# Hash-masked attention feeding an RWKV channel mix: second pair in query halves, third pair turned by TensorE, PSUM banks written out per operation, a new written sequence

## The chip, the cores and the metric

The kernel runs on one core of a Trainium2 chip (trn2). The metric is the device time of one execution in microseconds. The kernel before was timed three times: 250.73, 250.70 and 248.66 us, median 250.7.

Engines are named as in the profile: PE (matrix products), PEld (its weight loads), DVE (vector), ACT (scalar, activations), POOL (GpSimd), SP (here a queue that issues DMAs). PSUM is the accumulator memory that PE writes: 8 banks of 512 float32 a partition.

## The reference, cut to what matters

```python
# q, k, v: 4 batches x 8 heads x 768 positions x 64; proj: 64 x 6
q_bucket = sum over 6 bits of (q @ proj > 0) * 2**bit          # the same for k
scores = where(q_bucket == k_bucket, q @ k.T / 8, -1e9)
attn = exp(scores - max) / (sum + 1e-9)
x = (attn @ v) with the 8 heads side by side                   # 4 x 768 x 512
x_prev = x shifted by one position, zeros first
xk = mu_k * x + (1 - mu_k) * x_prev                            # xr the same with mu_r
out = sigmoid(xr @ w_r) * (relu(xk @ w_k) ** 2 @ w_v)          # w_k 512x1024, w_v 1024x512, w_r 512x512
```

## The kernel before

**Tiling.** Two heads make a pair; there are 16 pairs, four to a batch, and the channel mix (MoE in the names) of a batch runs once its four pairs are done. The code builds a list of operations with data dependencies (`add`, L144); a list of numbers, `ORDER` (L70), says in which sequence they are written, and each engine executes its own in that sequence, waiting where a dependency asks for it. `WHERE` (L40) gives the engine of the operations that may run on several. `Plan.schedule` (L199) walks through `ORDER` with estimated costs in order to choose PSUM banks: scores take a pair of banks out of three pairs, everything else one of banks 7 to 3.

**A pair, step by step.** The names in quotation marks are those of the operations; n is the pair.

- "ldq", "ldv": SP loads q and k (`nat`) and v (`vn`).
- "hi", "lo": q and k are split into two 16-bit halves, side by side in `nh`. For pairs in `FIRSTS` (0 and 1) it is done head by head, 384 columns a time (hi L616 on ACT or L618, lo L621); for the others 768 at a time (hi L554 or L556, lo L559). lo reads `nat` and the hi half of `nh`.
- Turning `nh` into `a` (64 + 64 rows, positions along the columns): for pairs in `FIRSTS` by six PE transposes a head ("t", L635) and a copy out of PSUM ("evt", L639); for the others by two DMA transposes ("tr", L563), issued by SP.
- The bucket bits: pair 0 has its own matmuls and evictions for each head and side ("b" L657, "beb" L663 on ACT, L665 on DVE). The others have 24 matmuls ("bits", L587), one eviction ("bx", L591) and 2 or 4 DMAs that carry the bits to rows of `a` ("row", L599, issued by SP). A score of equal buckets gets a constant that the exponential's bias takes off again.
- "sc" (L708): nine steps of 128 x 1024 scores; "exp" (L712): nine ACT exponentials into `pt`.
- "oo" (L736, L741): 72 matmuls of 65 columns, probabilities times v with a column of ones; "rc" (L751) and "ob" (L758) divide by the sum.
- The result is turned again, by PE ("ot" L794, copied out by "xt" L798) for pairs 0 to 3 and 15, by a DMA for the rest, then "xs", "xj" (shift by one), "df" L829, "xka", "xra" L837 and "xk", "xr" L841 form the mixed inputs on DVE.

Pairs in `HALVED` (2 and 3) run in two query halves: scores, "oo", "rc", "ob", "ot", "xt" and the mix are split, so that the first half of the positions goes on before the second.

**A batch's channel mix.** "kp" (L859, 16 groups of 4 matmuls of 384 columns), "relu" (L864 on ACT, L866 on DVE), "sq" (L869), "r" (L884) with "tanh" (L887), "v" (L896, eight matmuls of 512), "os" (L903) and the store "st" (L907). The last tile ("v3_5") is done in two column halves, lo and hi, which share a bank.

**Other things that are touched.** The weights come by "wl" (L447) and are cast by "wc" (L450 to L452). mu_k and mu_r are loaded element by element by ACT's queue (L422) and reduced by one on DVE (L424). v sums ("vsum", L509 to L515) and casts ("va", L501) run on POOL or DVE. Seven matmuls on zeros (L390) open PE's work.

Of the kernel before, what the change touches and what calls it, by code (L numbers as in the profile page):

```python
# [16 lines left out]

LAG = {"PE": 0.21, "ACT": 0.21, "DVE": 0.15, "POOL": 0.18, "SP": 1.8, "GQ": 2.0}
# [17 lines left out]
def R(kind, n):  # L36
# [33 lines left out]
ORDER = [  # L70
# [65 lines left out]
class Plan:  # L136
# [7 lines left out]
    def add(self, eng, dur, prio, fn, r=(), w=(), take=None, give=(), lag=None, name="", at=0.0, svc=0.0, off=None, tr=0, port=0, land=1.5):  # L144
# [31 lines left out]
        self.ops.append(o)  # L176
        return o

    def sequence(self):
        if ORDER:  # L180
            return [self.ops[i] for i in ORDER]
        left = {o.i: len(o.deps) for o in self.ops}
# [3 lines left out]
        while heap:  # L186
            o = self.ops[heapq.heappop(heap)[1]]
            seq.append(o)
            for s in o.succ:
                left[s] -= 1  # L190
                if not left[s]:
                    heapq.heappush(heap, (self.ops[s].prio, s))
# [772 lines left out]
```

## Time and profile before

| profiled execution | value |
|---|---|
| span, first to last instruction | 251.3 us (the three timed runs: median 250.7) |
| PE busy | 236.9 us, 94%, 2609 matmuls |
| DVE busy | 195.4 us, 78%, 471 instructions |
| ACT busy | 179.1 us, 71%, 225 instructions |
| POOL busy | 27.9 us, 11%, 73 instructions |
| chain that ended last | PE 75%, DMA 11%, DVE 8%, SP queue 3% |
| 144 exponentials (L712) | 138.8 us, 1040 ns each |
| 28 lo of 768 columns (L559) | 27.3 us, 976 ns each |
| 22 hi of 768 columns on DVE (L556) | 12.3 us, 557 ns each |

The profile is one execution. "Busy" is the time in which an engine had an instruction under way; idle time is put down to the instruction or DMA that released the next one. The chain is followed back from the last instruction, at each step to what released it.

### The profile page before, as it was taken

How to read it: one execution, taken by the hardware profiler on the slowest of the kernel's cores; microseconds unless marked ns; L12 is line 12 of the kernel's file. 1: busy time of each engine (PE TensorE's matmuls, PEld its weight loads, DVE VectorE, ACT ScalarE, POOL GpSimd, SP SyncE). 2: the span in 40 equal slices, each digit the busy share in tenths (PEclk: the TensorE clock that was granted, in tenths of full speed). 3: DMA queues.
4: the chain of work that ended last, by engine and by line, in shares of the span. 5: the costliest groups of instructions: out<-in, count | busy, mean ns of one | idle time of the engine just before them, and what ended most of it. 6: DMA issues, size and time to landing. Idle time of an engine off the chain costs nothing.

```text
span 251.3 us, 6510 instructions
## 1 busy us (share of the span) xinstructions
PE 236.9 (94%) x2609; PEld 147.6 (59%) x2609; DVE 195.4 (78%) x471; ACT 179.1 (71%) x225; POOL 27.9 (11%) x73
## 2 busy tenths in 40 slices
PE   6886799999799998999999999999999999999993
PEld 2444578876566655666467566655865654545442
DVE  3795679889788889898998999899787878376322
ACT  5596689999799978996878899988787223332220
POOL 5002240541302031100001100100000000000000
PEclk9799799999999999999999999999999999999998
DMA  6999999999989999999999996793231030022223
GB/s 187 308 178 251 220 215 191 267 249 189 213 292 241 204 293 292 273 201 269 184 333 186 184 185 158 210 230 57 90 64 44 0 128 28 13 83 86 83 85 125
DMA packets 75194, 44.56 MB, mean 177 GB/s; under 512 B 55524, under 2 KB 70172, under 8 KB 75164
## 3 DMA queue, kind: packets, MB, share of 16 engines
q1 hardware_dynamic: 74028, 44.15, 72.8%
q8 instruction: 20, 0.33, 0.6%
q10 hardware_dynamic: 1136, 0.01, 0.3%
q14 instruction: 10, 0.08, 0.1%
HBM read 24.12 MB, written 6.29 MB: 121 GB/s over the span
## 4 chain that ended last, share of the span: by engine, by line
PE 75%; DMA 11%; DVE 8%; SPq 3%; ACT 1%; issue 1%; DVEq 0%
PE ps_all L708 19%; PE ps_all L896 17%; PE ps_all L859 13%; PE ps_all L741 12%; PE ps_all L884 8%; DMA nat<-in_k_dram 5%; PE ps_all L587 4%; DMA nat<-in_q_dram 3%; DMA a<-bx 2%; DMA os<-in_moe_w_k_dram 1%; DVE nh L559 1%; DVE nh L556 1%; PE ps_all L736 1%; ACT pt L712 1%; PE ps_all L794 1%
## 5 line engine op out<-in xcount | busy, mean ns | idle before, releaser
L712 ACT ACTIVATE pt<-ps_all 128x1024 bf16<-128x1024 f32 x144 | 138.8, 1040 | 21.1 <-PE ps_all L708 19.8
L708 PE MATMUL ps_all<-a 128*128 128x512 f16 (+3 forms) x408 | 80.6, 318 | 5.1 <-DMA a<-bx 3.9
L708 PEld LDWEIGHTS <-a 128*128 128x128 f16 x408 | 35.3, 98 | 26.7 <-DMA a<-bx 4.7
L859 PE MATMUL ps_all<-xk,wk 128*128 128x384 bf16 x256 | 49.0, 326 | 0.9 <-DVE kr L866 0.9
L896 PE MATMUL ps_all<-wv,k 128*128 128x512 bf16 (+1 forms) x200 | 45.9, 370 | 0.6 <-DVE os L903 0.6
L741 PEld LDWEIGHTS <-pt 128*128 128x128 bf16 x1152 | 42.1, 98 | 6.9 <-issue 1.1
L741 PE MATMUL ps_all<-va,pt 128*128 128x65 bf16 x1152 | 43.9, 194 | 0.0
L859 PEld LDWEIGHTS <-wk 128*128 128x128 bf16 x256 | 24.5, 98 | 17.6 <-issue 1.6
L896 PEld LDWEIGHTS <-k 128*128 128x128 bf16 x200 | 19.4, 98 | 20.6 <-issue 0.7
L864 ACT ACTIVATE kr<-ps_all 128x384 bf16<-128x384 f32 x33 | 15.8, 493 | 19.2 <-DVE k L869 12.7
L887 ACT ACTIVATE rs<-ps_all 128x512 f32<-128x512 f32 x24 | 14.2, 603 | 20.9 <-PE ps_all L884 19.0
L559 DVE SCALAR_TENSOR_TENSOR nh<-nat,nh 128x768 f16<-128x768 f32 x28 | 27.3, 976 | 1.1 <-ACT nh L554 0.6
L903 DVE SCALAR_TENSOR_TENSOR os<-rs,ps_all 128x512 f32<-128x512 f32 (+1 forms) x25 | 16.5, 662 | 14.7 <-PE ps_all L896 9.9
L869 DVE TENSOR_TENSOR k<-kr 128x384 bf16<-128x384 bf16 x64 | 21.5, 350 | 3.7 <-ACT kr L864 3.5
L884 PE MATMUL ps_all<-wr,xr 128*128 128x512 bf16 x96 | 23.8, 379 | 0.0
L866 DVE TENSOR_SCALAR kr<-ps_all 128x384 bf16<-128x384 f32 x31 | 17.1, 555 | 8.3 <-PE ps_all L859 6.6
L758 DVE TENSOR_TENSOR ob<-ps_all,rc 128x384 bf16<-128x384 f32 (+1 forms) x36 | 18.3, 511 | 1.0
L884 PEld LDWEIGHTS <-xr 128*128 128x128 bf16 x96 | 9.0, 98 | 10.0 <-ACT kr L864 0.3
L587 PE MATMUL ps_all<-a,p0g 128*32 128x256 f16 (+1 forms) x180 | 13.4, 276 | 1.3 <-DMA a<-nh 1.3
L556 DVE TENSOR_SCALAR nh<-nat 128x768 f16<-128x768 f32 x22 | 12.3, 557 | 3.0 <-DMA nat<-in_q_dram 2.5
L587 PE MATMUL ps_all<-a,p1g 128*32 128x256 f16 (+1 forms) x180 | 12.9, 273 | 0.0
L841 DVE TENSOR_TENSOR xr<-tm,xt 128x768 bf16<-128x768 f16 (+1 forms) x18 | 9.4, 520 | 0.4
(94 smaller groups left out, 187.4 us busy)
## 6 DMA issues: line engine op xcount, KB each, us to landing
vn<-in_v_dram SPq DMA_DIRECT2D x16, 384.0 KB
out_dram<-os SPq DMA_DIRECT2D x23, 256.0 KB
nat<-in_k_dram SPq DMA_DIRECT2D x15, 384.0 KB
nat<-in_q_dram SPq DMA_DIRECT2D x15, 384.0 KB
wst<-in_moe_w_k_dram SPq DMA_DIRECT2D x2, 512.0 KB
wst<-in_moe_w_r_dram SPq DMA_DIRECT2D x2, 512.0 KB
wst<-in_moe_w_v_dram SPq DMA_DIRECT2D x2, 512.0 KB
a<-bx SPq DMA_DIRECT2D x48, 9.0 KB
```

The source lines that it names most:

```text
L559: nc.vector.scalar_tensor_tensor(out=nh[:, :, D:P], in0=nat.rearrange("p j (c d) -> p (j c) d", d=D), scalar=QS, in1=nh[:, :, 0:D], op0=AL ...
L587: nc.tensor.matmul(ps[g_ * wid : (g_ + 1) * wid, 0:FW], w_[:, m_ - 1 - x : m_ - 1 - x + wid], a_t[sa][:, i, x % NFOLD * FW : (x % NFOLD + ...
L708: nc.tensor.matmul(ps[:, lo - s * STEP : hi - s * STEP], side_a["k"][sa][:, j, jc * P : (jc + 1) * P], side_a["q"][sa][:, j, q0 : q0 + hi ...
L712: nc.scalar.activation(out=pt_t[sp][:, s * STEP : (s + 1) * STEP], in_=ps_t[plan.slot[nm]], func=AF.Exp, bias=EBIAS, scale=ESC)
L741: nc.tensor.matmul(oo[:, (ic - c0) * 65 : (ic - c0) * 65 + 65], pt_t[sp][:, o : o + P], va_t[sa][:, j, jc, 0 : D + 1], start=(not uc and i ...
L758: nc.vector.tensor_tensor(out=ob_t[so][:, c0:c1, j * D : (j + 1) * D], in0=oo[:, :, 0:D], in1=rc_t[sr][:, 1, c0:c1].unsqueeze(2).to_broadc ...
L859: nc.tensor.matmul(ps[:, 0:HALF], wk_sb[:, d, fc * P : (fc + 1) * P], xk_t[mx[d]][:, h * HALF : (h + 1) * HALF], start=(d == 0), stop=(d = ...
L866: nc.vector.tensor_scalar(out=kr_t[sk], in0=sm(nm)[:, 0:HALF], scalar1=0.5 ** 0.5, scalar2=0.0, op0=ALU.mult, op1=ALU.max)
L869: nc.vector.tensor_tensor(out=k2_t[s2][:, h * HALF : (h + 1) * HALF], in0=kr_t[sk], in1=kr_t[sk], op=ALU.mult)
L884: nc.tensor.matmul(sm(nr), xr_t[mx[d]][:, c * P : (c + 1) * P], wr_sb[:, d, :], start=(d == 0), stop=(d == NDC - 1))
L896: nc.tensor.matmul(sm(nv)[:, lo:hi], k2_t[(b * NFC + fc) % NK2][:, c * P : (c + 1) * P], wv_sb[:, fc, lo:hi], start=(fc == 0), stop=(fc == ...
L903: nc.vector.scalar_tensor_tensor(out=os_t[so][:, lo:hi], in0=rs_t[s1][:, lo:hi], scalar=1.0, in1=sm(nv)[:, lo:hi], op0=ALU.add, op1=ALU.mult)
```

## The change

Four parts, and a new `ORDER` and `WHERE` for all of it:

1. `HALVED` gets pair 1, `FIRSTS` gets pair 2: its q and k are split head by head and turned by 24 PE transposes and four copies out of PSUM instead of two DMA transposes.
2. mu_k and mu_r are loaded as rows (8 x 128), turned by one small matmul against an 8 x 8 identity that POOL makes, and reduced by one from PSUM.
3. `Plan.schedule` no longer estimates anything: a table `SLOT` names the first bank of each operation that takes PSUM.
4. In the last tile, the first matmuls of column half hi are made to come after the first ones of half lo.

```diff
-    HALVED = (2, 3)
+    HALVED = (1, 2, 3)
-    FIRSTS = (0, 1)
+    FIRSTS = (0, 1, 2)
...
+BANKS = {"sc": 2, "s3": 3, "sm": 1}
+SLOT = {
+    "warm": 7, "mu": 6, "t0q00": 6, "b0q00": 6, "t0q01": 7, "b0q01": 7, "t0k00": 5, "b0k00": 6, "t0k01": 4, "b0k01": 4, "t0q10": 7, "b0q10": 2,
...
+}
...
+        used, held = set(), {}
+        order = [self.ops[i] for i in ORDER]
         for o in order:
...
             if o.take is not None:
...
+                name, size = o.take[1], BANKS[o.take[0]]
+                self.slot[name] = SLOT[name]
+                held[name] = set(range(SLOT[name], SLOT[name] + size))
...
-    for t, src, key in ((muk, moe_mu_k, "muk"), (mur, moe_mu_r, "mur")):
...
-                nc.scalar.dma_start(out=t, in_=src.rearrange("(c p) -> p c", p=P))
...
+    add("POOL", 0.3, -2.2, lambda: make_identity(nc, id8), w=["id8"], name="id8")
+    for i_, src in enumerate((moe_mu_k, moe_mu_r)):
+        add("ACT", 0.42, -19.0, lambda i_=i_, src=src: nc.scalar.dma_start(out=mu8[i_ * NDC : (i_ + 1) * NDC, :], in_=src.rearrange("(c p) -> c p", p=P)),
+            w=[("mu8", i_)], at=0.75, svc=0.05, off=1.5, land=1.05, name=f"ldmu{i_}")
+    add("PE", 0.12, 1.0, lambda: nc.tensor.matmul(sm("mu")[:, 0 : 2 * NDC], mu8, id8, start=True, stop=True),
...
-                        r=[("wv", fc) for fc in range(4 * g, 4 * g + 4)] + [("k2", (b * NFC + fc) % NK2, h) for fc in range(4 * g, 4 * g + 4) for h in (c // 3,)],
+                        r=[("wv", fc) for fc in range(4 * g, 4 * g + 4)] + [("k2", (b * NFC + fc) % NK2, h) for fc in range(4 * g, 4 * g + 4) for h in (c // 3,)] + ([(nv, 0)] if lo and g == 0 else []),
```

Switches that the diff also brings in (`ROWD`, `STEPS`, `NWARM2`, `ROW_ACT`) are empty or zero and give no instruction.

The new sequence, engine by engine, from the start up to the first scores of pair 1 (a number behind a star repeats; "p" stands for the small preparations of constants):

```
PE before:   warm*7 t0k10 t0q01 t0q00 t0q10 t0k01 t0k00 b0k10 b0q10 b0k00 b0k01 t1k10 b0q00 sc0_6 sc0_8 b0q01 t1q00
             sc0_7 t1k00 sc0_5 t1q10 sc0_3 sc0_2 bits1 sc0_1 sc0_4 sc0_0 bits2 sc1_0
PE after:    warm*7 t0k10 t0q10 b0k10 b0q10 t0q01 t0q00 t0k00 t0k01 b0q01 sc0_6 sc0_5 b0k01 t1k10 sc0_7 t1k00 b0q00
             t1q10 t1q00 sc0_4 b0k00 sc0_3 bits1 sc0_1 t2k10 t2k00 sc0_0 t2q10 t2q00 sc0_8 sc0_2 bits2 sc1_8
ACT before:  hi0q0 hi0q1 evt0k10 evt0q10 evt0k01 hi1k0 mur beb0k10 beb0k01 evt1k10 beb0k00 exp0_6 ... exp0_0 exp1_0
ACT after:   hi0q0 hi0k0 evt0q01 beb0k10 evt0k01 evt0k00 exp0_6 exp0_5 hi1q0 beb0k01 exp0_7 ldmu1 hi3 hi2k1 exp0_4
             exp0_3 exp0_1 evt2k00 exp0_0 exp0_8 exp0_2 ldmu0 exp1_8
DVE after:   hi0k1 lo0k1 hi0q1 lo0q1 evt0k10 evt0q10 lo0q0 lo0k0 beb0q10 hi2q0 hi1k1 lo2q0 beb0q01 lo1k1 lo1k0 evt0q00
             evt1k10 lo1q1 lo1q0 beb0q00 evt1k00 evt1q00 evt1q10 lo2k0 beb0k00 lo2k1 vsum0 bx1 lo2q1 evt2k10 lo3
             evt2q10 evt2q00 va2 bx2
POOL after:  p hi1k0 hi1q1 va0 p hi2q1 p hi2k0 p hi3 p va1
SP after:    k, q, k, q of pair 0 | q2 k1 q1 v0 v2 k2 k3 v1 q3 k4 q4 v3 | row1*2 | k5 tr3 q5 row2*2 tr3 tr4*2
SP before:   k, q, q, k of pair 0 | k1 q2 k2 q1 q3 k3 tr2 q5 tr2 v0 q4 k4 | row1*2 | v1 v2 row2*2 tr3*2 k5
```

Over the whole kernel the operations change engines as follows: hi of 768 columns 22 on DVE, 6 on ACT, 0 on POOL become 10, 3 and 13; hi of 384 columns 5, 3 and 0 become 4, 4 and 4; vsum 30 on DVE and 18 on POOL become 15 and 33; relu 31 on DVE and 33 on ACT become 34 and 30; weight casts 4 on DVE, 2 on ACT, 4 on POOL become 2, 0 and 8. Copies out of PSUM after PE transposes of q and k are 5 on DVE and 5 on ACT before, 10 and 4 after. In the first batch's channel mix 14 of the 16 relu are DVE's, where 7 were.

At the end of the kernel PE's last operations are, before, v3_3, r3_3, r3_5, v3_4, then lo and hi of v3_5; after, lo and hi of v3_5 come first and the second half of v3_4 is last, with r3_4 between. The store of v3_1 is issued by SP after the first one of v3_5; v3_4's output uses the same buffer as v3_1's.

More of the change, by code (lines that the diff above doesn't have):

```diff
@@ L177, in add @@
         return o
[L179 to L182, printed above, removed]
-        heap = [(o.prio, o.i) for o in self.ops if not left[o.i]]
-        heapq.heapify(heap)
-        seq = []
[L186 to L192, printed above, removed]
-        return seq
@@ L195, in moved @@
-    @staticmethod
-    def moved(t, work):
-        return t + work * (1.25 if t < 9.3 else 1.0)
-    def schedule(self):
-        free = {e: 0.0 for e in ("PE", "ACT", "DVE", "POOL", "SP")}
-        bank_free = [0.0] * 8
-        used = [False] * 8
-        count = {"sc": 0, "sm": 0, "moe": 0}
-        held = {}
-        dma_free = tr_free = after = 0.0
-        port = [0.0, 0.0]
-        queue = []
-        order = self.sequence()
+    def schedule(self):
+        used, held = set(), {}
+        order = [self.ops[i] for i in ORDER]
@@ L209, in schedule @@
         for o in order:
-            e = "POOL" if o.eng == "GQ" else o.eng
-            if o.svc and o.eng != "GQ":
-                queue.append(o)
-            t = max([free[e], o.at] + [queue[-9].vis if o.svc and o.eng != "GQ" and len(queue) > 8 else 0.0] + [self.ops[d].own if self.ops[d].eng == o.eng and not self.ops[d].svc else self.ops[d].vis for d in o.deps])
             if o.take is not None:
-                cls, name, moe = o.take
-                if count[cls] >= self.most[cls] or (moe and count["moe"] >= self.moe_most):
+                name, size = o.take[1], BANKS[o.take[0]]
@@ L221, in schedule @@
-                held[name] = (cls, bs, moe)
-                for b in bs:
-                    used[b] = True
-                count[cls] += 1
-                count["moe"] += moe
-            o.start = t
-            dur = o.dur
-            if o.port:
-                dur += max(0.0, port[e == "DVE"] - t)
-                port[e != "DVE"] = t + dur
-            if e == "SP":
-                dur += after
-                after = 0.3 * o.tr
-            if o.tr:
-                dma_free += 0.5 * (dma_free > t)
-                dur = max(dur, dma_free - 1.0 - t, tr_free + 0.1 - t)
@@ L237, in schedule @@
-            o.took = dur
-            free[e] = t + dur
-            lag = o.lag
-            if o.svc:
-                first = max(t + o.off, dma_free)
-                dma_free = self.moved(first, o.svc)
-                lag = max(0.9, dma_free + o.land - t - dur)
-                if o.tr:
-                    tr_free = dma_free
-            o.own = t + dur + 0.1 * (e in ("DVE", "ACT"))
-            o.vis = t + dur + lag
-            for name in o.give:
-                cls, bs, moe = held.pop(name)
-                for b in bs:
-                    used[b] = False
-                    bank_free[b] = o.vis
-                count[cls] -= 1
-                count["moe"] -= moe
@@ L255, in schedule @@
-        self.end = max(o.start + o.took for o in order)
+                used |= held[name]
+            for name in o.give:
+                used -= held.pop(name)
         return order
@@ L324 @@
     bx_t = [buf([P, S // NFOLD], FP16, f"bx{i}") for i in range(NBX)]
+    if ROWD:
+        bdp = ctx.enter_context(tc.tile_pool(name="bd", bufs=1, space=bass.MemoryType.DRAM))
+        bd_t = [bdp.tile([P, FW], FP16, name=f"bd{i}", tag=f"bd{i}") for i in range(NBX)]
     vn_t = [buf([P, 2, HALF], FP32, f"vn{i}") for i in range(NV)]
@@ L389 @@
     for i in range(NWARM):
-        add("PE", 0.43, -20.0 + 0.1 * i, lambda: nc.tensor.matmul(sm("warm"), wz[:, 0:P], wz, start=True, stop=True),
-            r=["wz"], w=["warm"], take=("sm", "warm", 0) if i == 0 else None, give=["warm"] if i == NWARM - 1 else [])
+        add("PE", 0.2155, -20.0 + 0.1 * i, lambda: nc.tensor.matmul(sm("warm"), wz[:, 0:P], wz, start=True, stop=True),
+            r=["wz"], w=["warm"], take=("sm", "warm", 0) if i == 0 else None, give=["warm"] if i == NWARM - 1 else [], name="warm")
+    for i in range(NWARM2):
+        add("PE", 0.2155, -7.5 + 0.15 * i, lambda: nc.tensor.matmul(sm("warm2"), wz[:, 0:P], wz, start=True, stop=True),
+            r=["wz"], w=["warm2"], take=("sm", "warm2", 0) if i == 0 else None, give=["warm2"] if i == NWARM2 - 1 else [], name="keep")
     add("ACT", 1.5, -9.5, lambda: nc.scalar.activation(out=tb[:, 0:1], in_=tb[:, 1:2], func=AF.Exp), r=["tb"], w=["tb0"], at=0.75, name="table")
@@ L418 @@
                 px[:, 0 : NB * m_].rearrange("p (b f) -> p b f", f=m_)[:, :, m_ - 1], pp[:, 0:NB]), r=[key], w=[(key, g_)], name=f"c{key}{g_}")
[L419 to L425 removed]
+    add("POOL", 0.3, -2.2, lambda: make_identity(nc, id8), w=["id8"], name="id8")
[3 more added lines that the diff above has]
+    add("PE", 0.12, 1.0, lambda: nc.tensor.matmul(sm("mu")[:, 0 : 2 * NDC], mu8, id8, start=True, stop=True),
+        r=["id8", ("mu8", 0), ("mu8", 1)], w=[("mu",)], take=("sm", "mu", 0), name="mu")
+    add("DVE", 0.08, 1.3, lambda: nc.vector.tensor_scalar(out=mu_t, in0=sm("mu")[:, 0 : 2 * NDC], scalar1=-1.0, scalar2=None, op0=ALU.add),
+        r=[("mu",)], w=["muk", "mur"], give=["mu"], name="muv")
     wlist = [("k", c, 1) for c in range(NDC)] + [("r", 0, 2), ("r", 2, 2)] + [("v", c, 2) for c in range(0, NFC, 2)]
@@ L596, in add_bits, with bo, rd, row @@
         add("DVE", DVE_C(FW), R("bx", n), g, r=[(nm,)], w=[("bx", sx)], give=[nm], name=f"bx{n}")
+        if n in ROWD:
+            def bo():
+                nc.sync.dma_start(out=bd_t[sx], in_=bx_t[sx])
+            def rd():
+                nc.sync.dma_start(out=a_t[sa][D : D + NB, :, :], in_=bd_t[sx].rearrange("(g r) c -> g r c", g=4)[:, 0 : NB * m_, :].rearrange("g (b x) c -> b g (x c)", x=m_))
+            add("SP", 0.45, R("row", n) - 0.1, bo, r=[("bx", sx)], w=[("bd", sx)], svc=0.25, off=1.0, land=0.8, name=f"bo{n}")
+            add("SP", 0.55, R("row", n), rd, r=[("bd", sx)], w=[("ab", side, sa, j, h) for side in "qk" for j in range(2) for h in range(2)],
+                svc=0.25, off=1.1, land=0.9, name=f"rd{n}")
+            return
         for g_ in range(ng):
-            def row(g_=g_):
-                nc.sync.dma_start(out=a_t[sa][D : D + NB, g_ * 4 // ng : (g_ + 1) * 4 // ng, :], in_=bx_t[sx][g_ * wid : g_ * wid + NB * m_, :])
-            add("SP", 0.72, R("row", n) + 0.01 * g_, row, r=[("bx", sx)], w=[("ab", "qk"[i // 2], sa, i % 2, h) for i in range(g_ * 4 // ng, (g_ + 1) * 4 // ng) for h in range(2)],
+            on = "ACT" if (n, g_) in ROW_ACT else "SP"
+            def row(g_=g_, e=nc.scalar if on == "ACT" else nc.sync):
+                e.dma_start(out=a_t[sa][D : D + NB, g_ * 4 // ng : (g_ + 1) * 4 // ng, :], in_=bx_t[sx][g_ * wid : g_ * wid + NB * m_, :])
+            add(on, 0.75, R("row", n) + 0.01 * g_, row, r=[("bx", sx)], w=[("ab", "qk"[i // 2], sa, i % 2, h) for i in range(g_ * 4 // ng, (g_ + 1) * 4 // ng) for h in range(2)],
                 svc={1: 0.3, 2: 0.2, 4: 0.17}[ng], off=1.15, land=1.5, name=f"row{n}")
```

51 lines of the change are left out of this document (24 added, 27 removed), and 199 rows, old and new, of tables (ORDER, SLOT, WHERE).

## The prediction

> **What bounds the kernel now.** First the busy time by stretches of 10 us (after the stretch's length: busy us and instructions of PE, PEld, DVE, ACT, POOL, then granted clock, DMA share, GB/s).
>
> ```profile
> 0.00:10.00 10.00, 7.37 (x38) 3.38 (x39) 4.66 (x12) 5.35 (x9) 3.72 (x25) 0.86 0.80 246
> 10.00:20.00 10.00, 8.50 (x76) 4.93 (x75) 9.61 (x18) 8.41 (x11) 0.00 (x0) 0.97 0.96 199
> 20.00:30.00 10.00, 6.09 (x55) 3.76 (x54) 6.22 (x10) 5.71 (x7) 2.75 (x4) 0.89 0.95 245
> 30.00:40.00 10.00, 9.99 (x155) 7.76 (x154) 6.95 (x16) 8.74 (x11) 2.64 (x7) 0.94 0.94 228
> ...
> 60.00:70.00 10.00, 8.66 (x146) 5.78 (x139) 8.37 (x23) 8.63 (x11) 2.79 (x7) 1.00 1.03 226
> ...
> 80.00:90.00 10.00, 9.74 (x119) 6.22 (x117) 8.62 (x20) 9.58 (x13) 3.29 (x5) 1.00 1.10 230
> 90.00:100.00 10.00, 8.99 (x108) 5.28 (x110) 8.74 (x23) 7.20 (x10) 1.15 (x5) 1.00 1.13 272
> 100.00:240.00 140.00, 140.00 (x1423) 83.83 (x1413) 113.00 (x282) 94.05 (x124) 5.20 (x11) 1.00 0.59 141
> ```
>
> From 100 to 240 us PE has no idle time, and a batch's groups of eight 512-column matmuls follow at 0.216 us each (the chain has eight in 1.73 us), so nothing that DVE, ACT or POOL gains there is worth anything. PE's idle time is 2.63 + 1.50 + 3.91 us in the first 30 us, 1.34 + 0.26 + 1.01 = 2.6 us between 60 and 100, and the tail. So the sum is made of when PE's dense work begins, and of those holes.
>
> Then, around the largest hole: ACT by time, SP's queue by time, and the chain of waits.
>
> ```profile
> 13.81 1.02 ACT L712 ACTIVATE pt<-ps_all 128x1024 bf16<-128x1024 f32 x1 [0.60 <-PE ps_all L708]
> ...
> 27.27 3.97 ACT L712 ACTIVATE pt<-ps_all 128x1024 bf16<-128x1024 f32 x4 [3.95 <-PE ps_all L708]
> 32.40 35.28 ACT L712 ACTIVATE pt<-ps_all 128x1024 bf16<-128x1024 f32 x38 [1.17 <-PE ps_all L708]
> ```
>
> ```profile
> 12.17 1.55 SPq L563 DMA_TRANSPOSE a<-nh  x1
> ...
> 15.62 2.04 SPq L563 DMA_TRANSPOSE a<-nh  x1
> ...
> 20.45 2.36 SPq L599 DMA_DIRECT2D a<-bx  x2
> ```
>
> ```profile
> 22.07 4.43 DMA a<-bx
> 26.63 1.70 PE ps_all L708 x7
> ```
>
> Pair 0's exponentials start at 13.81 and end at 23.3; pair 1's bit rows, issued at 20.45, land only at 26.5, so scores, PE and ACT stand still for 4 us. After 32.4 ACT runs 38 exponentials in 35.28 us, 0.928 each, with no gap. PE is as full there: the 10 us from 40 hold 105 matmuls of 65 columns, 12 of 384, 18 of 256 and so on, which at the later stages' pace make 9.7 us. Hence a lead won before 27 us is kept by both engines.
>
> **Part by part.**
>
> *Pair 2 by PE, DMA side.* Two transposes leave SP's queue (3.6 us of issue) and the DMA queues: the trace's packets of 256 B between 12 and 20 us, 3,072 of them, took 4.8 us of all 16 queues. Ahead of row1 the new queue has twelve whole loads of 384 KB after pair 0's four halves, before it was eight and the transposes. By the packets a load takes 1.1 to 1.2 us, so pair 0 (2.2 us) and twelve loads (13.8) from 2.4 us on are through at 18.4. The last of them wait for buffers: k4 and q4 for pair 1's lo (about 12.4 and 14.4 below), v3 for va0 on POOL. Moved ahead of row1 are k4, q4 and v1 to v3; each of the last three adds 1.15 us if it slips past 18. Row1, issued at bx1, then meets empty queues: landing some 2 us later, 22.
>
> *First exponential.* q of head 1 comes second instead of third. DVE by its rows: k lands 3.2; hi, lo (0.36 + 0.56) to 4.15; q at 4.4, hi, lo to 5.4; two copies of 768 columns (0.55 each) and PE's transposes to 6.7; bits by PE (12 matmuls in 3.50 us, so 1.2 for 768 columns twice) to 8.4; beb0q10 0.955 to 9.4. On ACT evt0q01 (0.48, waits for a transpose behind those bits) stands ahead of beb0k10 (0.80), then two more copies of 0.48: first exp at 11.0, where it was 13.81.
>
> *ACT until pair 1.* Nine exps at 0.928 are 8.4; between them hi1q0 and hi2k1 (0.52 each), beb0k01 0.48, hi3 0.85, evt2k00 0.80, two issues at 0.4: 4.0. ACT could be free at 23.4, as before: the earlier start is spent on work that was elsewhere.
>
> *DVE until pair 1.* From 9.4: hi 2 x 0.36, lo 7 x 0.56, beb 3 x 0.555, evt 0.35 + 4 x 0.552, vsum 0.56, bx 0.42 = 9.85, so bx1 ends at 19.3 (before 20.4). Then lo2q1 0.56, evt2k10, evt2q10, evt2q00 0.55 each, lo3 0.96: 22.4, and bits2, written ahead of pair 1's scores, waits for that: 1.45 us, so sc1_8 at 24.05 and its exp at 24.5, against 27.27: **-2.8 us**. The 24 added transposes are 4 x 0.51 = 2.0 us of PE, and lie in its waits for DVE between 18 and 22; without that cover they cost 2.0.
>
> *Clock.* The granted clock is 0.89 and 0.94 from 20 to 40 us, 1.00 after. Without the hole it should stay up; 6% of 10 us, with the 1.17 us gap on ACT that falls into it: **-0.6** (0 to -1.2).
>
> *Pair 1 halved.* 36 matmuls of other cuts, the same columns; on DVE two more rc (0.18), ob 4 x 0.356 for 2 x 0.555, five mix steps in halves (0.15 more each), xt: 1.7 us of DVE, in a stage where DVE is at 0.70 to 0.89. No part of the batch's first product can start before pair 3, so: 0.
>
> *Engines.* hi moved off DVE and ACT, vsum and casts: DVE loses 12 x 0.56 + 15 x 0.4 + 2 x 0.69 = 14 us and gains 2.5 (evt), 1.7 (relu), 1.7 (halves), 0.9 (lo, beb); ACT loses 7. POOL gains 13 hi: the trace has none there. The nearest rows are a cast of 768 (0.93) and a two-input add of 390 (0.85, so 1.7 for 768); the kernel's own table writes 2.15. I take 1.7, and half for 384 columns. Worth 0 in time, as PE bounds.
>
> *Holes from 60 to 100 us.* The batch's new order decides them, which no row shows: between -2.6 (all gone) and +2.5 (as much again). I take **-0.6**. DVE's 14 relu for 7 are 3.9 us more there, hi and vsum moved away 5.
>
> *mu, SLOT.* One matmul; the element loads cost only 4-byte packets, 0.02 us in 2. Banks: in the first 40 exponentials one takes the bank pair just left by its predecessor; it costs one scores step, 0.45 us, where PE is not ahead. 0.
>
> *Tail.* PE waits 0.57 us for DVE between lo and hi; that goes. But the last eviction has 512 columns (0.69 for 0.42), its store double the bytes, and it waits for v3_1's store, issued late by SP: v3_4 cannot leave before that lands. **+0.5** (-0.3 to +1.5).
>
> Sum: 251.3 - 2.8 - 0.6 - 0.6 + 0.5 = 247.8. The median of the runs is 0.6 below the profiled span: **247.2**.
>
> **Rivals.**
>
> *A, the forecast* (0.45): 245.9 to 248.6.
>
> *B, the later holes go too* (0.20): 2.0 more of them, 245.2. For it: they are waits for one bit matmul's transpose and one relu chain, and DVE is emptier. Against: nothing in the code aims at them by name.
>
> *C, the lead is given back at 60 to 100 us* (0.20): 14 relu on DVE in series with "sq", or POOL's long casts late for the weights, widen the holes by 2.5: 250.3. For it: the wait of PE for L866 is 0.9 us already. Against: DVE falls by 7 us over the kernel.
>
> *D, POOL and DVE block each other in the opening* (0.15): slower. The trace has it once:
>
> ```profile
> 27.62 0.99 POOL L501 CAST va<-vn 128x768 bf16<-128x768 f32 x1 [2.28 <-DMA vn<-in_v_dram]
> 27.97 1.46 DVE L559 SCALAR_TENSOR_TENSOR nh<-nat,nh 128x768 f16<-128x768 f32 x1
> ```
>
> lo takes 0.96 alone, and 1.46 when it starts under a POOL cast: it begins when that ends. POOL idles from 10 to 20 us now; the change puts four hi and va0 there, 4 x 0.85 + 0.93 = 4.3 us at my value and 5.9 at the table's 1.25, among seven lo that DVE needs in order, and behind each stands all of DVE's queue: beb0q00, bx1, evt2. If every one of them is added to DVE, bx1 ends at 23.6 to 25.2, and pair 1 starts at 28.8 to 30.4. From 2.8 us of such waits the lead is gone; with 5.9, and 0.9 more from two such collisions later, 254.0. Against it: beside POOL's other casts DVE mostly kept its usual times, having started first, and POOL gave way (a copy of 254 columns took 1.06).
> The Trainium skill (SBUF — State Buffer, Who interferes with whom) has this as a rule against such a move: GpSimd and a DVE instruction with two SBUF inputs share a port pair under an exclusive lock, and whichever comes second is blocked for the whole of the other. The 1.46 agrees.
> The Trainium skill (GPSIMD Engine Reference, Engine selection) also says that GpSimd is about half as fast as DVE with two inputs, yet near line rate with one. By that hi would cost what the cast row gives, 0.47 for 384 columns, the five operations 2.8 us, and D would end at 250.0, no slower than before; no row has hi on POOL, so I keep the dearer price.
>
> **Numbers.** One per cent (2.5 us) is what a measurement here can tell from none: the three runs spread over 2.1. Faster than 248.2: A 0.38, B 0.20, C 0.03 = 0.61. Within: A 0.07, C 0.16, D 0.02 = 0.25. Slower than 253.2: D 0.13, C 0.01 = 0.14. Range: down to B with its bounds (244.4), up through C (251.5) into D's mild form, 252.0; left out are some 0.05 below and 0.13 above.
>
> **What would show it.** Right: first exponential at about 11 us, 9 of them and the ACT extras done by 24, pair 1's first exponential at 24 to 25 with its rows landed before, no wait for "a<-bx" over 1 us in the chain, clock at 1.00 from 25 us on, PE without idle time after 100 us. D would show lo rows of 1 us and more beside POOL's hi in the first 25 us. C would show PE waits for "kr" or "wk". Wrong altogether if PE's rows in 30 to 60 us turn out to have had slack: then the lead is lost or doubled there.

## The result, and the profile after

The change makes the kernel slower: 256.6 us median (255.46 to 257.2, four runs) against 249.84 for the kernel before on the same chip (248.66 to 250.73, four runs), a ratio of 1.0333 with a 95% interval of 1.0259 to 1.0406. Forecast were 247.2 us, and 244.4 to 252.0.

The profiled execution of the changed kernel took 256.96 us, with a span of 255.2. First its busy time by stretches, in the columns of the prediction's first view (start and end, length, then busy us and instructions of PE, PEld, DVE, ACT, POOL, granted clock, DMA share, GB/s).

```profile
0.00:10.00 10.00, 8.45 (x44) 3.96 (x45) 5.82 (x13) 4.16 (x8) 3.42 (x21) 1.00 0.80 244
10.00:20.00 10.00, 8.09 (x81) 4.51 (x80) 9.75 (x20) 8.27 (x12) 9.37 (x15) 1.00 0.90 309
20.00:30.00 10.00, 9.73 (x154) 7.57 (x151) 8.01 (x13) 8.94 (x10) 5.91 (x9) 1.00 0.84 152
...
60.00:70.00 10.00, 8.92 (x160) 6.75 (x157) 9.96 (x25) 9.41 (x12) 5.01 (x5) 1.00 1.18 224
...
90.00:100.00 10.00, 8.93 (x129) 5.89 (x129) 8.84 (x22) 7.15 (x10) 2.05 (x3) 1.00 0.80 149
100.00:170.00 70.00, 65.62 (x805) 41.40 (x812) 60.17 (x140) 57.27 (x66) 29.08 (x22) 1.00 0.82 199
```

The first three lines are what the change had to win, and it won it: the clock is 1.00 from the start, and PE works 9.73 us between 20 and 30 where it worked 6.09. The last line is where the largest part of the loss lies. PE, which had no idle time there before, stands 4.4 us of those 70, and no other engine is full either (DVE 60.2, ACT 57.3 of 70), nor are the DMA queues (0.82): what PE waits for changes from place to place. Five waits make 3.7 of the 4.4 us; most of the rest lies beside matmuls whose records are missing from this trace (18 of 2649).

Then ACT by time, around the opening's landmarks:

```profile
10.29 1.96 ACT L707 ACTIVATE pt<-ps_all 128x1024 bf16<-128x1024 f32 x2
...
22.69 1.04 ACT L707 ACTIVATE pt<-ps_all 128x1024 bf16<-128x1024 f32 x1
24.62 9.27 ACT L707 ACTIVATE pt<-ps_all 128x1024 bf16<-128x1024 f32 x10 [0.89 <-PE ps_all L703]
34.42 6.52 ACT L707 ACTIVATE pt<-ps_all 128x1024 bf16<-128x1024 f32 x7 [0.53 <-PE ps_all L703]
```

The first exponential comes at 10.29 (13.81 before), and pair 1's start 0.89 us after pair 0's have ended, where ACT stood 3.95 us.

PE's two longest waits behind 100 us (time of start and length, then in brackets the wait ahead of it and who ended it), and the end of the chain of waits:

```profile
111.05 0.59 PE L891 MATMUL ps_all<-wv,k 128*128 128x512 bf16 x2 [1.53 <-POOL wv L433]
...
111.91 1.03 PE L891 MATMUL ps_all<-wv,k 128*128 128x512 bf16 x4
...
114.39 0.81 PE L891 MATMUL ps_all<-wv,k 128*128 128x512 bf16 x3 [1.02 <-DVE wv L434]
```

```profile
246.55 1.32 PE ps_all L891 x12
...
249.16 2.13 DMA out_dram<-os
```

PE waits for weights that POOL and DVE cast late, and at the end the last eviction waits for an earlier store, as the prediction had it: from PE's end to the end of the span it is 4.7 us, before 3.2.

The groups of POOL and DVE that carry the split of q and k (count, busy us, mean ns, then the idle time before):

```profile
L539 POOL TENSOR_SCALAR nh<-nat 128x768 f16<-128x768 f32 x13 | 30.3, 2335 | 21.9 <-DMA nat<-in_q_dram 12.4 <-DMA vn<-in_v_dram 5.3 <-issue 2.9
L542 DVE SCALAR_TENSOR_TENSOR nh<-nat,nh 128x768 f16<-128x768 f32 x26 | 29.4, 1133 | 4.1 <-POOL nh L539 4.0
```

hi costs POOL 2335 ns, and lo on DVE went from 976 to 1133. DVE, from which work was taken, is busy 198.0 us in place of 195.4: added up over all its operations, those that ran longer than their kind beside POOL's work account for about 15 us, before for 2.4.

PE's idle time, added up from its instructions in each trace (us), from its first matmul at 1.2 us on. "Before again" is the first run below: the kernel before once more, with a time of 249.1 near the median. The last two columns are experiments told below.

| stretch | before, as predicted from | before again | changed | p4b_all_fair | c500_new_to_70us |
|---|---|---|---|---|---|
| 0 to 30 | 6.86 | 4.00 | 2.56 | 3.31 | 3.22 |
| 30 to 60 | 0.01 | 0.01 | 1.57 | 0.27 | 0.73 |
| 60 to 100 | 2.61 | 1.89 | 2.59 | 3.01 | 2.88 |
| 100 to 170 | 0.00 | 0.32 | 4.38 | 0.67 | 0.00 |
| 170 to PE's end | 0.57 | 0.99 | 0.47 | 1.68 | 1.68 |
| from PE's end to the span's | 3.23 | 3.23 | 4.74 | 3.29 | 3.42 |

Changed against before again: -1.4 in the opening, then +1.6 + 0.7 + 4.1 - 0.5, +1.5 at the end, and 2.1 more of busy PE (237.7 for 235.6, the added transposes mostly): +8.1 of rounded terms, where the spans differ by 255.2 - 247.3 = 7.9. Each column is one execution. In the five other traces of the new sequence (experiments below) PE stands 3.0 to 7.2 us between 100 and 170 us; in the twelve with before's sequence and engines there, 0 to 1.5.

### The profile page after: what moved, and what is told of

It is laid out like the page before. It is cut to its first block, busy times and chain, and to the rows that moved or that the text cites. A ratio compares the mean times of both kernels' runs of the same rounds, so it can differ in the third digit from the quotient of the medians.

```text
span 255.2 us, 6620 instructions
## 1 busy us (share of the span) xinstructions
PE 237.7 (93%) x2631; PEld 149.2 (58%) x2649; DVE 198.0 (78%) x462; ACT 173.4 (68%) x217; POOL 81.9 (32%) x110
## 4 chain that ended last, share of the span: by engine, by line
PE 47%; DMA 17%; DVE 11%; POOL 7%; ACT 7%; issue 5%; SPq 4%; DVEq 0%; POOLq 0%
PE ps_all L891 13%; PE ps_all L854 13%; PE ps_all L703 8%; ACT pt L707 7%; PE ps_all L879 6%; DMA a<-nh 5%; PE ps_all L736 4%; POOL nh L539 3%; DMA wst<-in_moe_w_k_dram 3%; DMA nat<-in_k_dram 3%; DMA nat<-in_q_dram 2%; DMA k<-in_moe_w_v_dram 2%; PE ps_all L570 2%; SPq L594 2%; DVE nh L542 2%
## 5 line engine op out<-in xcount | busy, mean ns | idle before, releaser
L736 PEld LDWEIGHTS <-pt 128*128 128x128 bf16 x1152 | 43.2, 97 | 7.4 <-issue 1.3
L736 PE MATMUL ps_all<-va,pt 128*128 128x65 bf16 x1152 | 45.5, 193 | 0.5 <-DVE va L517 0.5
L539 POOL TENSOR_SCALAR nh<-nat 128x768 f16<-128x768 f32 x13 | 30.3, 2335 | 21.9 <-DMA nat<-in_q_dram 12.4
L542 DVE SCALAR_TENSOR_TENSOR nh<-nat,nh 128x768 f16<-128x768 f32 x26 | 29.4, 1133 | 4.1 <-POOL nh L539 4.0
L859 ACT ACTIVATE kr<-ps_all 128x384 bf16<-128x384 f32 x30 | 14.3, 492 | 21.5 <-PE ps_all L854 12.2
L864 DVE TENSOR_TENSOR k<-kr 128x384 bf16<-128x384 bf16 x64 | 22.3, 369 | 5.7 <-ACT kr L859 5.4
L861 DVE TENSOR_SCALAR kr<-ps_all 128x384 bf16<-128x384 f32 x34 | 18.5, 550 | 7.0 <-PE ps_all L854 6.4
L492 POOL TENSOR_TENSOR vt<-vn 128x384 f32<-128x384 f32 x6 | 6.3, 1048 | 25.1 <-DMA vn<-in_v_dram 24.8
```

The source lines that it names most:

```text
L539: e.tensor_scalar(out=o, in0=x, scalar1=QS, scalar2=None, op0=ALU.mult)
L542: nc.vector.scalar_tensor_tensor(out=nh[:, :, D:P], in0=nat.rearrange("p j (c d) -> p (j c) d", d=D), scalar=QS, in1=nh[:, :, 0:D], op0=AL ...
L736: nc.tensor.matmul(oo[:, (ic - c0) * 65 : (ic - c0) * 65 + 65], pt_t[sp][:, o : o + P], va_t[sa][:, j, jc, 0 : D + 1], start=(not uc and i ...
L861: nc.vector.tensor_scalar(out=kr_t[sk], in0=sm(nm)[:, 0:HALF], scalar1=0.5 ** 0.5, scalar2=0.0, op0=ALU.mult, op1=ALU.max)
L864: nc.vector.tensor_tensor(out=k2_t[s2][:, h * HALF : (h + 1) * HALF], in0=kr_t[sk], in1=kr_t[sk], op=ALU.mult)
```

## The experiments

Ratios are to the kernel before, with 95% intervals. `ORDER` and `SLOT` are shown by the names of their operations; where a sequence is put together from the two, `SLOT` is given out anew for it.

**The kernel before, again** (no edit).

> The kernel before, once more, for its trace. Theory (cold profile): the profile I argued from was an execution whose granted clock was low at the start (0.86 in the first 10 us, 0.983 on the whole), while the typical one is not; then this one has 0.99 to 1.00 in the first 40 us, a span of 247 to 249 us, and the wait of PE for pair 1's bit rows before 27 us is at most 2 us. Rival (the opening as I read it): clock under 0.95 in the first 10 us again, span about 251, the wait at 22.1 us again 4 us long.

249.11 us, span 247.3, clock 0.985. Neither: the clock was as low as in the first profile, but the wait for pair 1's rows was half as long.

```profile
0.00:10.00 10.00, 7.26 (x38) 3.41 (x39) 5.85 (x15) 5.42 (x9) 3.96 (x25) 0.89 0.80 249
10.00:20.00 10.00, 9.69 (x81) 5.43 (x79) 9.26 (x16) 8.44 (x12) 0.00 (x0) 0.94 1.05 238
20.00:30.00 10.00, 7.86 (x92) 5.30 (x92) 5.92 (x10) 6.63 (x8) 3.20 (x4) 0.83 0.99 240
```

```profile
24.14 1.97 PE L708 MATMUL ps_all<-a 128*128 128x512 f16 x7 [2.14 <-DMA a<-bx]
```

Three more runs below have before's opening, and the same wait: 2.01, 1.77 and 2.23 us. The 3.91 from which the forecast was made is the outlier of five.

**POOL's hi back, then its sums and casts too.**

```diff
-    "hi3q": "POOL", "hi4q": "POOL", ... "hi11k": "POOL", "hi13q": "POOL", "hi15k": "POOL",
+    "hi3q": "DVE", "hi4q": "DVE", ... "hi11k": "ACT", "hi13q": "ACT", "hi15k": "ACT",
```

> The changed kernel with the 13 hi of 768 columns that POOL runs put back on the engines that they had before (10 on DVE, 3 on ACT); order and banks stay as changed. Theory 1 (POOL's hi are dear): 13 operations of 2.1 to 2.9 us leave the chains from load to bit rows, and lo goes back from 1.13 to 0.98 us; at least 3 us of the 6.7 come back, ratio to before 1.02 or less. Theory 2 (weights late and order): PE's waits for the v weights near 109 and 113 us stay, 1 us or less comes back, ratio 1.027 or more. Theory 3 (DVE is needed): DVE is full from 50 to 70 us, and 10 more hi there make it slower than the changed kernel, ratio 1.037 or more.

1.0579 (1.0506 to 1.0652): slower than the changed kernel by 2.4 per cent. The trace shows a place in the sequence that is bad for it. ACT by time at the worst of it:

```profile
128.50 0.60 ACT L885 ACTIVATE rs<-ps_all 128x512 f32<-128x512 f32 x1
133.40 0.84 ACT L540 ACTIVATE nh<-nat 128x768 f16<-128x768 f32 x1 [4.30 <-DMA nat<-in_q_dram]
134.15 1.92 ACT L710 ACTIVATE pt<-ps_all 128x1024 bf16<-128x1024 f32 x2
```

The hi had been written early, for POOL, where nobody stands behind it while it waits for its load. In ACT's queue the exponentials stand behind it: PE then waited 4.59 us for ACT.

> As the run before, and the 22 sums of v and the casts of the weights wc0, 3, 5, 6, 7 also back on the engines of before. Theory 1: POOL was the whole loss but for 1 to 2 us; ratio 1.00 to 1.012, and the stretch of DVE's operations beside POOL's falls from 15 us to under 4. Theory 2: the waits for the v weights (1.53 and 1.02 us) go with the casts, so 2 to 3 us more than in the run before come back. Theory 3: DVE, now as loaded as before, gets late in the stages from 50 to 110 us; no faster than the changed kernel.

1.0512 (1.0437 to 1.0586). The waits for the v weights went, as theory 2 has it, but others of 1.52 and 2.60 us came at 125 and 131 us. DVE's lengthening beside POOL fell to about 4 us in this run. Both runs are marred by such places, and settle no price.

**mu and the last store.**

```diff
 ORDER, places:
-ldmu1 92 ... ldmu0 148 ... id8 181 ... os3_1 1391 ... st3_1 1409
+ldmu1 92, ldmu0 93 ... id8 126 ... os3_1 1391, st3_1 1392
```

> The changed kernel with four places of the written sequence altered: the second row load of mu right behind the first, the identity for mu right behind the big identity on POOL, and the store of v3_1 right behind its product. If the wait of PE at 30.2 us (0.78) and the store that the last product waits for (tail 4.7 us after PE's end, before 3.2) are losses of their own: 1.3 to 2.3 us back, ratio 1.024 to 1.028, and the tail falls to 3.5 or less. If mu's 0.78 is cover for something else that is late by then: 0.9 or less, from the tail alone.

1.0326 (1.0259 to 1.0392): no gain that can be measured. In the trace mu's wait fell from 0.78 to 0.44 us and the tail from 4.7 to 3.9, but PE waited 2.12 us for DVE at 64.6, which it had not in the changed kernel's trace.

**The parts in before's sequence.** Only mu, the rule of the last tile and the table of banks remain:

```diff
-    HALVED = (1, 2, 3)
+    HALVED = (2, 3)
-    FIRSTS = (0, 1, 2)
+    FIRSTS = (0, 1)
-ORDER, WHERE: the new ones
+ORDER, WHERE: those of before; mu at the place where mu_k was reduced
```

> The changed code with the pairs of before (HALVED 2 and 3, FIRSTS 0 and 1) and before's written sequence and engines: what is left of the change is mu by PE, the rule for the last tile, and the banks as a table. Theory S (the new sequence and its engines lose the time): ratio 0.995 to 1.01, the tail as long as before's. Theory P (the parts themselves cost): mu's wait of 0.8 us on PE and a longer tail show here, ratio 1.01 to 1.015.

1.0031 (0.9993 to 1.0069); PE waits 0.75 us at 33 us for mu's identity. The tail is 3.2 us: the rule of the last tile does not lengthen it, the new sequence does.

> As the run before, but with pair 1 in two query halves too, its pieces at the places of before's whole ones. Theory S: within 1 us of the run before. Theory P: 1.7 us more of DVE in a stretch where it is full, so 1.5 to 3 us slower than the run before.

1.0153 (1.0101 to 1.0205), theory P by the number, but by a place again. PE by time:

```profile
35.78 0.60 PE L694 MATMUL ps_all<-a 128*128 128x256 f16 x4
37.61 0.25 PE L722 MATMUL ps_all<-vsu,tiny 128*128 128x195 bf16 x1 [1.23 <-ACT pt L698]
37.70 0.28 PE L727 MATMUL ps_all<-va,pt 128*128 128x65 bf16 x4
38.53 0.63 PE L727 MATMUL ps_all<-va,pt 128*128 128x65 bf16 x15 [0.55 <-ACT pt L698]
```

The second half's products stood where whole pair 1's had stood, directly behind the scores whose exponentials they need. Moved behind two more score steps:

```diff
 ORDER: score steps of PE between the last one needed and the product
-oo1_0_3, first and second: 0
+oo1_0_3, first and second: 2
```

> Pair 1 in halves again, in before's sequence, but its second half's products are written after the exponentials that they need (in the run of it before, two of them were written with no score step in between, and PE stood 1.23 + 0.55 us at 36 us for ACT). If the 2.6 us that the halves cost there were that place alone: within 1 us of the run without halves, ratio 1.000 to 1.007. If the halves themselves cost (DVE's 1.7 us): ratio 1.010 to 1.016.

1.0052 (1.0009 to 1.0094): 0.2 per cent above the run without halves, within its interval. By themselves the halves cost little or nothing.

Pair 2 by PE, pair 1 whole:

```diff
 p1_mu_tail with
-    FIRSTS = (0, 1)
+    FIRSTS = (0, 1, 2)
+ORDER, WHERE: places 0 to 149 of the new sequence, with its engines, then before's
```

> The changed code with pair 2 by PE (FIRSTS 0, 1, 2) but pair 1 whole; the first 150 places of the new sequence with their engines, then before's sequence and engines. The opening's lead by itself: the first exponential at about 10.3 us, pair 1's from 24.5 on. Theory S: the lead of 2 to 2.8 us is kept, ratio 0.987 to 1.00. Theory P: the 24 transposes and five more evictions cost PE and DVE as much as the opening wins, ratio 1.00 to 1.015.

1.0080 (1.0042 to 1.0118), theory P by the number. The trace shows a place where the lead is held up, DVE by time and then PE:

```profile
67.92 0.56 DVE L744 TENSOR_TENSOR ob<-ps_all,rc 128x384 bf16<-128x384 f32 x1
70.70 0.56 DVE L530 TENSOR_SCALAR nh<-nat 128x768 f16<-128x768 f32 x1 [2.23 <-DMA nat<-in_q_dram]
71.30 0.96 DVE L533 SCALAR_TENSOR_TENSOR nh<-nat,nh 128x768 f16<-128x768 f32 x1
72.17 0.55 DVE L852 TENSOR_SCALAR kr<-ps_all 128x384 bf16<-128x384 f32 x1
```

```profile
72.77 0.81 PE L845 MATMUL ps_all<-xk,wk 128*128 128x384 bf16 x4 [1.96 <-DVE kr L852]
```

The engines are ahead, the loads are not. DVE stands at a hi whose q has not landed, the first relu of the channel mix behind it, and PE behind the relu.

```diff
-hi8q lo8q ... relu0_0_0          -row6 x4 ... ldq8q
+relu0_0_0 hi8q lo8q              +ldq8q row6 x4
```

> Pair 2 by PE in before's sequence again; hi and lo of q of pair 8, which stood at the head of DVE's queue for 2.23 us waiting for their load, while the first relu of the channel mix waited behind them and PE for the relu (1.96 us at 70.8), are written behind the first relu, and the load ahead of pair 6's bit rows in SP's queue. If the opening's lead is lost at that place: PE's wait at 70.8 falls under 0.5 us, ratio 0.990 to 1.001. If the lead is lost to the transposes and evictions as such: the wait comes back at another place, ratio 1.004 to 1.012.

1.0007 (0.9963 to 1.0051): that wait is gone, and the part with its opening costs nothing. It wins nothing either. PE now stood 1.47 us at 38.5 for a bank pair that the exponential just before it still held; the next run took that away, too.

```diff
 SLOT
-sc1_5: 4, sc1_8: 0, sc2_2: 0, sc2_0: 2, ...
+sc1_5: 2, sc1_8: 4, sc2_2: 0, sc2_0: 2, ...      (14 entries)
```

> Pair 2 by PE in before's sequence, hi and lo of pair 8 behind the relu, and now 14 score steps on other pairs of PSUM banks, so that sc2_2 no longer follows sc1_8 in the same pair (PE stood 1.47 us at 38.5 us for that exponential, and ACT 0.74 after it). If the lead is lost to such places and no more: the stop goes and the ratio is 0.990 to 0.998, faster than both kernels. If what waits next takes it: ratio 0.998 to 1.004.

1.0008 (0.9967 to 1.0048). The stop went and the time did not move: the 18th exponential ends 1.7 us earlier than in the kernel before again (32.9 for 34.6), the 36th 0.8 (50.5 for 51.3), the 63rd at the same 78.2. No version that beats both kernels came out of this.

**All four parts in before's sequence.**

```diff
 p3_firsts with
-    HALVED = (2, 3)
+    HALVED = (1, 2, 3)
```

> All four parts, but only the first 150 places of the new sequence with their engines; the rest in before's sequence on before's engines, so that POOL has hardly any hi. Theory S: ratio 0.99 to 1.01, 6 us or more better than the changed kernel. Theory P: ratio 1.02 to 1.035, as the changed kernel.

1.0192 (1.0120 to 1.0263), with the halves at their bad places. With those mended, and scores taking the bank pairs in turn from 30 to 40 us:

```diff
-oo1_0_3, first and second: 0 score steps behind the last one needed
+oo1_0_3, first and second: 2
+SLOT given out anew, sc2_2 not behind sc1_8 in one pair
```

> All four parts of the change; the first 150 places of the new written sequence with their engines (about the first 25 us), then before's sequence and engines, pair 1's second half written where its exponentials are done, and scores that take PSUM's pairs in turn around 30 to 40 us. If the new written sequence behind place 150 loses the time (the channel mix written later: the last product of batch 0 stands behind 128 of the 144 score steps, before behind 93): ratio 0.997 to 1.010, channel-mix work on PE by 170 us 41 us or more (changed kernel 32, before 42). If the parts lose it together: ratio 1.02 or more.

1.0170 (1.0111 to 1.0229). Between the two theories: half of the loss is there, half is not. Two more places that its trace showed:

```diff
-hi8q lo8q ... relu0_0_0          -row6 x4 ... ldq8q          -sc14_3: 0, sc14_5: 2
+relu0_0_0 hi8q lo8q              +ldq8q row6 x4              +sc14_3: 2, sc14_5: 0
```

> All four parts, as in the first such run that is mended for pair 1's halves, with the two more places mended that its trace showed: hi and lo of pair 8 behind the first relus, its load ahead of pair 6's rows, and two score steps at 173 us on other banks (PE stood 1.11 us there). If the 1.7 per cent of all parts in before's sequence are such places: ratio 1.003 to 1.012. If the parts cost together what they don't cost alone: 1.014 to 1.022.

1.0219 (1.0112 to 1.0325). The mending did not take: PE waits 2.05 us at 77.8 for a relu, and the 1.11 at 172.5 is still there. So the parts together cost 1.7 to 2.2 per cent in that sequence, where those alone come to 0.5 (0.3 with mu, 0.2 for the halves, 0 for pair 2); which of it is a bad fit and which the parts' own work stays open.

**How far the new sequence is at fault.**

```diff
 p4b_all_fair
-ORDER, WHERE: places 0 to 149 of the new sequence, with its engines, then before's
+ORDER, WHERE: places 0 to 499 of the new sequence, with its engines, then before's
```

> The same, but the first 500 places from the new sequence with their engines (about 70 us, 59 of the 144 score steps, five of POOL's long hi), then before's. If the loss is made behind there, by the late channel mix: ratio 0.997 to 1.012, no more than 1 us of PE idle time from 100 to 170 us (changed kernel 4.4, before 0). If it is made from 25 to 70 us, by DVE full beside POOL's hi: ratio 1.018 or more.

1.0200 (1.0137 to 1.0263). By the number alone that is the second theory, but the 2.0 per cent were there before the stretch from 25 to 70 us was put in: against p4b_all_fair (1.0170) the new sequence costs nothing measurable from 25 to 70 us, though it puts four more of the long hi on POOL there and DVE is busy 35.8 us from 30 to 70 in place of 33.0. Behind 70 us it costs the rest, 1.3 per cent or 3.3 us by the two ratios, with some 1.0 per cent of uncertainty if both intervals are taken together. The profiled execution of this run is the fastest of its four (252.43 us, median 254.1). The stretch from 100 to 170 us, in this run and then in the kernel before:

```profile
100.00:170.00 70.00, 70.00 (x828) 43.83 (x826) 63.13 (x157) 59.73 (x71) 4.94 (x10) 1.00 0.94 214
```

```profile
100.00:170.00 70.00, 70.00 (x844) 44.08 (x834) 63.74 (x157) 59.87 (x71) 4.88 (x10) 1.00 0.98 220
```

PE is full in both, where the changed kernel has 65.62. What there is more of on PE is the channel mix. The v products alone (busy us and count on PE), before and changed:

```profile
100.00:170.00 70.00, 15.61 (x64) 1.00 0.98 220
```

```profile
100.00:170.00 70.00, 11.94 (x44) 1.00 0.82 199
```

By 170 us the kernel before had run 128 kp, 32 r and 64 v matmuls, the changed one 111, 23 and 44 (a few records are missing in its trace; e2b_hi_back_at_lo, which has them all and the same sequence but for 13 hi, shows 104, 30 and 48); c500_new_to_70us, where PE is full, had run 128, 40 and 66. The exponentials went the other way: the last one ends at 181.1, in the kernel before again at 190.3. The new sequence writes attention first and the channel mix behind it: the last v product of batch 0 stands behind 128 of the 144 score steps in place of 93. The reading that fits these counts: while attention goes on, at a pace that ACT, DVE and loads set together, PE lacks the work that filled its waits; the work is done after 181 us, where PE is full anyway. No run moves the channel mix forward by itself.

**Two causes that the trace offered, and that are not.** The weights:

```diff
 ORDER, places
-wl6 693, wl7 717, wl9 712, wl8 750, wc5 657
+wl6 604, wl7 605, wl9 645, wl8 646, wc5 616   (and the casts wc4, 6 to 9 earlier)
```

> The changed kernel with the loads of the four v weights written 60 to 100 places earlier in SP's queue, and the casts of the r and v weights earlier on POOL and DVE. Theory (weights late is a term of its own): PE's waits of 1.53 and 1.02 us at 109 and 113 go, and 1.5 to 3 us come back, ratio 1.015 to 1.025. Rival (those waits cover something else, loads of q and k that then come later): under 1 us, ratio 1.026 or more.

1.0355 (1.0278 to 1.0432). The two waits went, and PE waited 3.08 us at 102 for a bit row of `a`, behind the loads that now went first. What waits is replaced by what is next. And POOL's hi once more, each right ahead of its lo:

```diff
 e2_hi_back with, for each of the 13
-hi11q 691 ... lo11q 724
+hi11q lo11q
```

> The 13 hi of POOL on before's engines once more, but each written right ahead of its lo, so that it doesn't stand in an engine's queue waiting for its load (4.30 us of ACT's time at 129 us, in the run where they kept their places). Theory 1 (POOL's 2.1 to 2.9 us are dear): now 2 to 4 us better than the changed kernel, ratio 1.015 to 1.025. Theory 3 (this sequence needs the hi off DVE): 0 to 3 us worse than the changed kernel, ratio 1.033 to 1.045.

1.0315 (1.0255 to 1.0375), the same as the changed kernel within the intervals. In this sequence it does not matter who does these hi. DVE's lengthening beside POOL's other work stayed at about 14 us, so the run says nothing of what that costs. In before's sequence the same move does matter:

```diff
 before
-    "hi3q": "DVE", "hi4q": "DVE", ... (13 hi of 768 columns)
+    "hi3q": "POOL", "hi4q": "POOL", ...
```

> The kernel before, and of the change only the 13 hi of 768 columns that go to POOL, at their places in before's sequence. Theory (POOL's hi are dear where lo is written right behind): every lo waits 1.6 us longer than for DVE's hi, and DVE's queue with it; 13 times that, part of it hidden: ratio 1.015 to 1.05. Rival (the engine makes no difference, as in the changed kernel, where putting them back gained 0.2 per cent): ratio 0.995 to 1.008.

1.0355 (1.0277 to 1.0433): this edit costs as much as the whole change. It is not quite alone: before's code chooses the PSUM banks by estimated costs, and with the engines 65 of its bank choices changed as well. Some of the loss is place, as the first case shows, POOL by time and then PE:

```profile
16.74 2.13 POOL L559 TENSOR_SCALAR nh<-nat 128x768 f16<-128x768 f32 x1 [10.22 <-DVE a L668]
18.93 1.00 POOL L420 COPY p1g<-p 128x6 f16<-128x6 f16 x1
```

```profile
19.98 0.43 PE L590 MATMUL ps_all<-a,p1g 128*64 128x256 f16 x2 [1.99 <-POOL p1g L420]
```

A copy that pair 1's bit matmuls need stood behind a hi before which POOL had waited 10 us. How much of the 3.5 per cent is POOL's slowness, how much such places and how much the banks was not taken apart.

## Why the prediction was wrong

The forecast was a gain of 3.5 us on its own base of 250.7; measured were 6.8 us of loss. By the runs, 1.3 of the 3.3 per cent come with the new sequence behind 70 us. The other 2.0 are in c500_new_to_70us as well, and how they divide between the parts' own work and a sequence that does not fit them stays open.

- **Opening** (-2.8, and -0.6 for clock and gap): its events came as written. The first exponential was put at 11.0 and came at 10.29, ACT free at 23.4 (23.7), bx1's end at 19.3 (19.6), pair 1's exponentials at 24.5 (24.62), the clock at 1.00. The size was wrong: the hole that goes is 1.8 to 2.2 us in the four other traces that have it, not 3.9. The clock term was there in some executions only: in the profile the granted clock is 0.50 for 3.4 us behind the hole, but of the seven executions of the kernel before that were timed with the first experiments four had a mean clock of 0.999 or 1.000, which leaves no room for such a stretch. And the 24 transposes, put at nothing as lying in PE's waits, do not seem to be covered: PE is busy some 2 us more, and its idle time of the first 30 us fell by only 1.4 against the kernel before again.
- **"A lead won before 27 us is kept by both engines"**: this step failed. The 18th exponential ends 1.7 us earlier than in the kernel before again, the 36th 1.0, the 54th 0.4, and the 63rd 0.2 later. These are single executions, and the two of the kernel before differ by 3.1 us at the 63rd; the firmer sign is that the runs with pair 2 by PE and the same opening end at 1.0007 and 1.0008 of before's time, where a lead of 1.7 us that is kept would be 0.993. ACT without a gap and a full PE were read as the only limits of 32 to 70 us; the run with pair 2 alone shows a third one, loads that keep their own time and engines that stand in order behind them.
- **"From 100 to 240 us PE has no idle time"**: true of before, and taken over for the changed kernel without a reason. The new sequence was allowed to move holes only between 60 and 100 (-2.6 to +2.5, taken -0.6; measured 0.0 to +0.7, inside). It made 4.4 us of new ones between 100 and 170. This is the largest missing term of the account, and no rival had it: C put the loss between 60 and 100 us and on relu and weights; of these only the casts' waits came, at 109 and 113 us, and taking them away gained nothing.
- **Engines** (hi at 1.7 us on POOL, "worth 0"): 2.34 each, and 1.26 for 384 columns where 0.85 was taken; DVE did not lose 7 us but gained 2.6, as its operations ran longer beside POOL's. In the changed kernel's sequence it was indeed worth 0 (1.0333 and 1.0315); in before's sequence the move costs 3.5 per cent. The Trainium skill (GPSIMD Engine Reference, Engine selection) has one-input work on GpSimd near line rate; this case's rows of 2.13 us and more against 0.557 on DVE contradict it for this operation.
- **Rival D**, the lock in the opening: 15 instructions, five hi among them, filled POOL to 9.37 us of 10, and bx1 came on time. Rows as the lock would make them come later: at 104.35 a lo beside a POOL cast and a hi took 1.79 us for 0.95, which agrees with the Trainium skill (SBUF — State Buffer, Who interferes with whom). DVE's rows that ran longer than their kind while POOL worked add up to about 15 us (2.4 before). What that costs in time is not shown: with hi taken off POOL both the time and the lengthening stayed, and the run in which the lengthening fell to about 4 us was slower still (1.0512), with the bad places that it has.
- **Halves 0, mu and banks 0**: right within 0.2 and 0.3 per cent, each alone. Together with pair 2 by PE the parts cost 1.7 to 2.2 per cent in a sequence not made for them.
- **Tail** (+0.5, to +1.5): +1.5 from PE's end to the span's, less the 0.57 that went; the store that waits is the mechanism that was named.
- **Span to time**: the median was taken as 0.6 below the profiled span. A run's time is 1.8 above its span, in both kernels (256.96 and 255.2, 249.11 and 247.3); so the execution profiled first was some 3 us slower than the median, and part of what it showed was not there to be won.

Not separated: behind 70 us c500_new_to_70us puts back sequence and engines at once (hi, sums of v and casts), and the channel mix was not moved forward by itself. So the late channel mix is the reading that the counts support, not one that a run of its own shows. POOL's work beside DVE is the rival. Against it: in e3_pool_back, with the new sequence, POOL is busy only 3.6 us from 100 to 170 us and DVE's lengthening there is under 1 us, yet PE stands 7.1 us, some 2.5 to 3 even without the two places named; and in c500_new_to_70us some 5 us of lengthening from 30 to 70 us cost nothing that can be measured.

## What to carry to other kernels

When a change replaces a sequence written by hand, treat the sequence as a part of the change with a price of its own. Before pricing the parts, count for each stage what stands ahead of what, above all how much work that waits for nothing is left to fill the bound engine; a stage that was full with the old filler need not be full with the new.
An operation that goes to another in-order engine needs a new place as well: early on an engine with nothing behind it, late where others queue.
Size a hole by more than one execution, and a lead by the first stage behind it that is fed just in time.

## What the runs showed of the hardware

The granted clock from 20 to 30 us was 0.83 in the three runs whose PE waited 2.01 to 2.23 us there, 0.89 with 3.91 us, and 1.00 in the one with 1.77 us. Taken in shorter stretches, it is 1.00, then 0.50 for 3.4 us, then 1.00 again: in the first profile from 27.7 us, in the kernel before again from 24.95, in p1_mu_tail from 24.6 and in h1_halved_fair from 23.8, so near the end of the wait each time. The same 0.50 for 3.4 us stands beside PE's waits of 4.59, 3.08, 2.12 and 1.99 us in e2_hi_back, w1_weights_early, e4_mu_tail and e6_before_hi_pool, and in p2_halved from 39.45 us, where three shorter waits (1.23, 0.55 and 0.62 us) lie close together; it does not stand beside the 2.60 us in e3_pool_back. An estimate from these numbers: at half the clock PE loses up to 1.7 us of those 3.4, so a wait of some 2 us can cost nearly twice its length.

POOL took 2.13 to 2.90 us to turn 768 float32 columns into float16 written 64 of every 128 (the changed kernel's trace), DVE 0.557 as the mean of 22 (before's trace).
